# Expert matmuls that read their moving columns and write their PSUM columns from last to first

## The chip, the cores and the metric

One NeuronCore of a Trainium2 chip runs the whole kernel in one launch. The metric is device time in microseconds (us). Three runs of the kernel before gave 1216.09, 1219.02 and 1219.22 us, median 1219.02.

## What is computed

Three layers follow each other over 8 x 576 = 4608 tokens of 512 features:

```python
kv = einsum('bhsd,bhse->bhde', softmax(k, axis=2), v)
x = einsum('bhsd,bhde->bhse', softmax(q, axis=-1), kv)      # linear attention, 8 heads of 64
top2 = the two largest of 8 noisy gate logits of each token
for e in range(8):                                          # mixture of experts
    h = maximum(x[mask] @ w1[e], 0)                         # 512 -> 1024
    out[mask] += top2_w[mask, None] * (h @ w2[e])           # 1024 -> 512
soft mixture of experts over out (32 slots, 8 experts)      # the last layer
```

Everything comes in and goes out as float32. The change touches the two products of the mixture of experts, `x @ w1[e]` and `h @ w2[e]`.

## The kernel before

The attention runs first, and its second half is mixed with the first expert blocks by a table of steps. The last layer (`tail`) stands behind the experts. Between them lies the expert stage: tokens are gathered by expert, in blocks of two or three pieces of 128 tokens that share one expert. `block(b, ...)` does one block in eight units `u`: units 0 to 3 are the first product (a quarter of the 1024 hidden columns each), units 4 to 7 the second (a quarter of its contraction each). In this data there are 35 blocks: 10 early pair blocks, 5 blocks of three pieces ("three-blocks", inside `tc.If`, for which the program holds 14) and 20 further pair blocks.

The products are computed nearly in float32 by splitting. Each operand is stored as a float32r part "h" and a rest "l" (`xh`, `xl`; `hh`, `hl`; `R0h`, `R0l` and so on for three buffers of weights), and each product is three matmuls: h with h, h with l, l with h. The split of a unit's weights (line 797, one ACT activation and one DVE subtraction over 1024 columns) runs two units ahead of their use, from a ring of float32 loads (`ringS`).

Three functions issue the matmuls; in each, the second argument is the stationary operand, which TensorE loads (PEld), and the third the moving one, of which it takes one column after another and writes one PSUM column for each:

- `hidden` (line 830): per unit 24 matmuls; the stationary operand is a 128 x 128 piece of weights, the moving one 256 token columns of `xh` or `xl`, the output half of a bank of `ph`. ACT (line 833) and DVE (line 834) then read `ph` to make `hh` and `hl`.
- `hidden1` (line 843), for the third piece of a three-block: 12 matmuls per unit with 128 tokens stationary and 256 columns of weights moving, the output one half of a bank of `ph`. The result goes through ACT and two transposes (line 849).
- `result` (line 860): the hidden values are stationary, 512 columns of weights move, the output is a whole bank of `py`. A pair block issues 12 matmuls per unit, a three-block 18. DVE (line 865) reads `py`, and an indirect DMA adds the rows to the output.

`xpose` (line 815) transposes the next block's gathered rows into a bank of `ph` in unit 6. All matmuls stand in one queue in program order. The banks of `ph` take turns, and an instruction that reuses a bank waits on semaphores of the engines that used it before; `PE_49` is the semaphore that TensorE's own instructions raise, `DVE_49`, `Activation_49` and `DMASWn_49` those of the others.

```python
for c in range(4):
    for (i, x) in ((0, xh), (0, xl), (1, xh)):
        nc.tensor.matmul(ph[:, g, :], w[i][:, c, g * P:(g + 1) * P], x[:, c, :], start=n == 0, stop=n == 11)
```

Of the kernel before, what the change touches and what calls it, by code (L numbers as in the profile page):

```python
# [21 lines left out]
P = 128  # L22
# [722 lines left out]
def experts(k, att, rs):  # L745

    nc, tc = k.nc, k.tc
    with ExitStack() as ctx:
# [6 lines left out]
        def bank(n, shape):  # L755
            b = banks[n]
            b.append(b.pop(0))
            return b[-1][0].tile(shape, F32, name=b[-1][1])
# [63 lines left out]
        def hidden(b, u):  # L822

            w = [x.rearrange("p (c f) -> p c f", c=4) for x in slot[b, u]]
            ph = bank("ph", [P, 2, 256])
            for g in range(2):
                n = 0
                for c in range(4):
                    for (i, x) in ((0, xh), (0, xl), (1, xh)):
                        nc.tensor.matmul(ph[:, g, :], w[i][:, c, g * P:(g + 1) * P], x[:, c, :], start=n == 0, stop=n == 11)  # L830
                        n += 1
            fs = slice(2 * u, 2 * u + 2)
            nc.scalar.activation(hh[:, fs, :], ph, AF.Relu)  # L833
            nc.vector.scalar_tensor_tensor(hl[:, fs, :], ph, 0.0, hh[:, fs, :].bitcast(F32), op0=ALU.max, op1=ALU.subtract)  # L834

        def hidden1(b, u):

            w = [x.rearrange("p (c f) -> p c f", c=4) for x in slot[b, u]]
            ph = bank("ph", [P, 2, 256])
            n = 0  # L840
            for c in range(4):
                for (i, x) in ((0, x3[0]), (0, x3[1]), (1, x3[0])):
                    nc.tensor.matmul(ph[:, 0, :], x[:, c, :], w[i][:, c, :], start=n == 0, stop=n == 11)
                    n += 1
            hr = yp.tile([P, 256], F32, name="hr")
            nc.scalar.activation(hr, ph[:, 0, :], AF.Relu)
            pt = bank("pt", [P, 4, P])
            for g in range(2):
                nc.tensor.transpose(pt[:, g, :], hr[:, g * P:(g + 1) * P], k.ident)
            fs = slice(2 * u, 2 * u + 2)  # L850
            nc.scalar.activation(h3[0][:, fs, :], pt[:, 0:2, :], AF.Copy)
            nc.vector.tensor_sub(h3[1][:, fs, :], pt[:, 0:2, :], h3[0][:, fs, :].bitcast(F32))

        def result(b, u, py):
            w = [x.rearrange("p (c f) -> p c f", c=2) for x in slot[b, u]]
            order = [(f, s) for f in range(2) for s in range(len(py))]
            for f, s in order if u < 7 else sorted(order, key=lambda x: x[1]):
                a = [x[:, 2 * (u - 4) + f, s * P:(s + 1) * P] for x in (hh, hl)] if s < 2 else [x[:, 2 * (u - 4) + f, :] for x in h3]
                for (n, (h, i)) in enumerate(((0, 0), (0, 1), (1, 0))):
                    nc.tensor.matmul(py[s], a[h], w[i][:, f, :], start=u == 4 and f == n == 0, stop=u == 7 and f == 1 and n == 2)  # L860

        def scatter(b, s, py):
            y = yp.tile([P, D], F32, name="y", bufs=3)
# [8 lines left out]
        def block(b, n_s, n, n_n):  # L872
# [8 lines left out]
            for u in range(8):  # L881
                split(*ahead[u])
                if u == 0:
                    load(n, 0)
                    load(n, 1)
                if u < 6:
                    load(n, ahead[u][1])
                if u < 4:
                    hidden(b, u)
                    if n_s == 3:  # L890
                        hidden1(b, u)
                else:
                    if u == 4:
                        py = [bank(f"py{s}", [P, D]) for s in range(n_s)]
                    if u == XU:
                        for s in range(n_n):
                            xpose(n, s)
                    result(b, u, py)
                if u == 1:
                    finish()  # L900
                    nc.vector.tensor_copy(gc, gn)
                yield
# [501 lines left out]
```

## Time and profile before

| | |
|---|---|
| Median of three runs | 1219.02 us (1216.09 to 1219.22) |
| Profiled execution, its own time | 1222.69 us |
| Its span, first to last instruction | 1221.0 us |
| Granted TensorE clock, mean | 0.967 |
| PE busy | 1125.1 us (92%) |
| DVE busy | 799.3 us (65%) |
| ACT busy | 570.8 us (47%) |
| POOL busy | 324.6 us (27%) |
| HBM traffic | 240 GB/s over the span |

The profiled execution took 1.69 us more than its span and 3.67 us more than the median of the runs. "PE" is the matmul itself and "PEld" the load of the stationary operand, which overlaps it. The duration of one matmul in the records runs from its first column to the modelled end of its last, so back-to-back matmuls overlap in the records; what a matmul costs in a stream is the distance from start to start, which the pieces of the chain give (length of a piece over its count).

### The profile page before, as it was taken

To read this page: it belongs to the slowest core of one execution; us is meant where nothing else is said; L and a number is where in the kernel's file an instruction comes from. 1 tells how busy PE (TensorE), PEld (TensorE's weight loads), DVE (VectorE), ACT (ScalarE), POOL (GpSimd) and SP (SyncE) were. 2 spreads that over 40 slices of the span, in tenths; PEclk is the share of its full clock that TensorE was granted. 3 is DMA by queue.
4 is the path that set the end of the run, shared out by engine and by line. 5 is a ranking of instruction groups with operands and counts; after the bars stand their busy time and mean duration, and the time that the engine had idled before them with its cause. 6 is when DMAs were issued, how large, how long until landed. Compare 5 with 4: busy or idle time off the path is not lost. (4 is left out here: it accounts for less than half of the span.)

```text
span 1221.0 us, 21167 instructions
## 1 busy us (share of the span) xinstructions
PE 1125.1 (92%) x7804; PEld 984.7 (81%) x7804; DVE 799.3 (65%) x1383; ACT 570.8 (47%) x877; POOL 324.6 (27%) x348
## 2 busy tenths in 40 slices
PE   2898859999999999999989999999999999969994
PEld 1787759998889999888968998998998998956542
DVE  7899778666976665554546666666666666645653
ACT  3575355465544544334434454544454454424324
POOL 4442153222244222211223322322321321210000
PEclk8899779999999999999999999999999999988997
DMA  9998162875536566555667564563745253237797
GB/s 327 297 318 306 45 207 77 242 227 157 141 84 189 135 199 172 139 149 163 174 184 249 138 202 106 150 195 84 223 110 173 47 148 84 43 66 295 265 356 310
DMA packets 116104, 219.08 MB, mean 179 GB/s; under 512 B 13968, under 2 KB 54032, under 8 KB 111888
## 3 DMA queue, kind: packets, MB, share of 16 engines
q1 hardware_dynamic: 98944, 177.11, 42.3%
q0 software_dynamic: 17040, 40.44, 16.8%
q8 instruction: 67, 1.10, 0.4%
q14 instruction: 53, 0.43, 0.1%
HBM read 243.31 MB, written 49.70 MB: 240 GB/s over the span
## 5 line engine op out<-in xcount | busy, mean ns | idle before, releaser
L797 DVE TENSOR_TENSOR R1l<-ringS,R1h 128x1024 fp32r<-128x1024 f32 x96 | 117.8, 1227 | 105.8 <-ACT R1h L797 103.3
L797 DVE TENSOR_TENSOR R0l<-ringS,R0h 128x1024 fp32r<-128x1024 f32 x95 | 116.8, 1229 | 100.8 <-ACT R0h L797 100.5
L797 ACT ACTIVATE R1h<-ringS 128x1024 fp32r<-128x1024 f32 x96 | 101.9, 1061 | 144.3 <-PE py L860 85.1
L797 DVE TENSOR_TENSOR R2l<-ringS,R2h 128x1024 fp32r<-128x1024 f32 x91 | 112.0, 1231 | 84.1 <-ACT R2h L797 81.7
L797 ACT ACTIVATE R0h<-ringS 128x1024 fp32r<-128x1024 f32 x95 | 100.8, 1061 | 137.9 <-PE py L860 77.0
L797 ACT ACTIVATE R2h<-ringS 128x1024 fp32r<-128x1024 f32 x91 | 96.5, 1061 | 136.2 <-PE py L860 75.1
L830 PE MATMUL ph<-xl,R0h 128*128 128x256 f32 x400 | 111.7, 279 | 1.5 <-issue 1.5
L830 PE MATMUL ph<-xh,R0h 128*128 128x256 f32 x400 | 112.0, 280 | 1.0 <-DVEq L949 1.0
L830 PE MATMUL ph<-xh,R0l 128*128 128x256 f32 x400 | 111.5, 279 | 0.0
L834 DVE SCALAR_TENSOR_TENSOR hl<-ph,hh 128x512 fp32r<-128x512 f32 x140 | 95.7, 684 | 23.2 <-ACT hh L833 23.2
L830 PE MATMUL ph<-xh,R1h 128*128 128x256 f32 x360 | 101.1, 281 | 8.1 <-DVE sc L820 7.6
L742 POOL DMA_INDIRECT xg<-xtab,pl_idx x40 | 50.3, 1257 | 215.9 <-DVE sc L820 197.6
L830 PE MATMUL ph<-xh,R2h 128*128 128x256 f32 x360 | 100.9, 280 | 0.5 <-DVE hl L834 0.5
L830 PE MATMUL ph<-xl,R1h 128*128 128x256 f32 x360 | 100.7, 280 | 0.0
L830 PE MATMUL ph<-xh,R1l 128*128 128x256 f32 x360 | 100.5, 279 | 0.0
L830 PE MATMUL ph<-xl,R2h 128*128 128x256 f32 x360 | 100.5, 279 | 0.0
L830 PE MATMUL ph<-xh,R2l 128*128 128x256 f32 x360 | 100.3, 279 | 0.0
L866 POOL DMA_INDIRECT x<-y,pl_idx x40 | 64.1, 1602 | 127.9 <-DVE y L865 117.8
L833 ACT ACTIVATE hh<-ph 128x512 fp32r<-128x512 f32 x140 | 81.6, 583 | 31.7 <-PE ph L830 31.7
L860 PE MATMUL py<-R1l,hh 128*128 128x512 f32 x200 | 79.7, 398 | 0.0
L860 PE MATMUL py<-R1h,hl 128*128 128x512 f32 x200 | 79.0, 396 | 0.0
L830 PEld LDWEIGHTS ph<-xh,R0h 128*128 128x128 f32 x400 | 75.7, 189 | 2.3 <-issue 1.6
(441 smaller groups left out, 3011.0 us busy)
## 6 DMA issues: line engine op xcount, KB each, us to landing
ringS<-in_moe_w_dram SPq DMA_DIRECT2D x292, 512.0 KB
ringA<-in_moe_w_dram SPq DMA_DIRECT2D x12, 1024.0 KB
ringA<-in_moe_w_dram SPq DMA_DIRECT2D x22, 512.0 KB
xtab<-xr SPq DMA_DIRECT2D x36, 256.0 KB
kt<-in_k_dram SPq DMA_DIRECT2D x8, 1024.0 KB
v<-in_v_dram SPq DMA_DIRECT2D x8, 1024.0 KB
x<-z SPq DMA_DIRECT2D x5, 1280.0 KB
ringS<-x SPq DMA_DIRECT2D x5, 1024.0 KB
```

The source lines that it names most:

```text
L742: k.nc.gpsimd.indirect_dma_start(out=x, out_offset=None, in_=k.xtab[:n], in_offset=bass.IndirectOffsetOnAxis(ap=idx, axis=0))
L797: turn[1:] = [nc.scalar.activation(r[0], f, AF.Copy), nc.vector.tensor_sub(r[1], f, r[0].bitcast(F32))]
L830: nc.tensor.matmul(ph[:, g, :], w[i][:, c, g * P:(g + 1) * P], x[:, c, :], start=n == 0, stop=n == 11)
L833: nc.scalar.activation(hh[:, fs, :], ph, AF.Relu)
L834: nc.vector.scalar_tensor_tensor(hl[:, fs, :], ph, 0.0, hh[:, fs, :].bitcast(F32), op0=ALU.max, op1=ALU.subtract)
L860: nc.tensor.matmul(py[s], a[h], w[i][:, f, :], start=u == 4 and f == n == 0, stop=u == 7 and f == 1 and n == 2)
L866: d = nc.gpsimd.indirect_dma_start(out=k.x2[:NTOK // 2] if b < NPA else k.x2, out_offset=bass.IndirectOffsetOnAxis(ap=at(b, s), axis=0), i ...
```

## The change

All operands keep their places, sizes and types, and no instruction is added to the products or taken away. In the three functions the moving operand and the output get a step of -1 along the columns: column 255 (or 511) of the moving operand enters first and is written to PSUM column 255 (or 511), and so on down to column 0. Both being turned, every value lands where it did. The stationary operands, the transposes and all readers of PSUM are as before. In the built program these operands start at column 255 (or 511) with a step of -1.

```diff
@@ hidden, line 830
-                        nc.tensor.matmul(ph[:, g, :], w[i][:, c, g * P:(g + 1) * P], x[:, c, :], start=n == 0, stop=n == 11)
+                        nc.tensor.matmul(ph[:, g, ::-1], w[i][:, c, g * P:(g + 1) * P], x[:, c, ::-1], start=n == 0, stop=n == 11)
@@ hidden1, line 843
-                    nc.tensor.matmul(ph[:, 0, :], x[:, c, :], w[i][:, c, :], start=n == 0, stop=n == 11)
+                    nc.tensor.matmul(ph[:, 0, ::-1], x[:, c, :], w[i][:, c, ::-1], start=n == 0, stop=n == 11)
@@ result, line 860
-                    nc.tensor.matmul(py[s], a[h], w[i][:, f, :], start=u == 4 and f == n == 0, stop=u == 7 and f == 1 and n == 2)
+                    nc.tensor.matmul(py[s][:, ::-1], a[h], w[i][:, f, ::-1], start=u == 4 and f == n == 0, stop=u == 7 and f == 1 and n == 2)
```

The order of the instructions is the same on all five engines. What the tracking of dependences adds are waits of TensorE on its own semaphore, four in each three-block and none elsewhere. On PE, in a three-block, the first matmul of `hidden` in unit 2 follows the last two of `hidden1` of unit 1:

```order
 L843 MATMUL ph_4576<-R1h,x3l 128x256
 L843 MATMUL ph_4576<-R1l,x3h 128x256
-L830 MATMUL ph_4600<-xh,R2h 128x256
+L830 MATMUL ph_4600<-xh,R2h 128x256 [waits PE_49]
 L830 MATMUL ph_4600<-xl,R2h 128x256
 L830 MATMUL ph_4600<-xh,R2l 128x256
```

The new wait is for the last matmul of `hidden1` of unit 0, which used the same bank; 38 matmuls lie between it and the waiting one. Unit 3 has the same.

On PE, in unit 6 of a three-block, the first transpose into a bank of `ph`:

```order
 L860 MATMUL py_4702<-R1l,h3h 128x512
 L860 MATMUL py_4702<-R1h,h3l 128x512
-L815 MATMUL ph<-ident,xg_1731 128x128 [waits DMASW3_49]
+L815 MATMUL ph<-ident,xg_1731 128x128 [waits DMASW3_49,PE_49]
 L815 MATMUL ph<-ident,xg_1731 128x128 x3
 L815 MATMUL ph_4753<-ident,xg_1737 128x128 [waits DMASW4_49,DVE_49]
```

Here the wait is for the last matmul of `hidden1` of unit 2, more than 50 matmuls earlier, and since the instruction now waits for two semaphores, one of the waits stands in an instruction of its own ahead of it. The transposes of the third piece have the same.

Waits of this kind stand in the program before as well. On PE, at the start of `hidden1` of unit 0 in the same block:

```order
L830 MATMUL ph_4499<-xh,R0l 128x256
L843 MATMUL ph_4526<-R0h,x3h 128x256 [waits PE_49,Activation_49]
L843 MATMUL ph_4526<-R0h,x3l 128x256 [waits DVE_49]
L843 MATMUL ph_4526<-R0l,x3h 128x256
L843 MATMUL ph_4526<-R0h,x3h 128x256
```

This piece is the same before and after.

## Rows read from the trace of the kernel before

**Rows 1.** The page: busy time, share, instructions; granted clock in 40 slices.

```profile
PE 1125.1 (92%) x7804; PEld 984.7 (81%) x7804; DVE 799.3 (65%) x1383; ACT 570.8 (47%) x877; POOL 324.6 (27%) x348
...
PEclk8899779999999999999999999999999999988997
```

**Rows 2.** Busy time by stretch of 100 us, columns named in the second line.

```profile
core 0: us, PE busy (x) PEld busy (x) DVE busy (x) ACT busy (x) POOL busy (x), PEclk, DMA share, GB/s
200.00:300.00 100.00, 99.75 (x670) 89.47 (x670) 66.10 (x113) 50.94 (x80) 30.66 (x35) 1.00 0.70 209
700.00:800.00 100.00, 100.00 (x663) 90.88 (x663) 64.70 (x89) 49.76 (x62) 26.26 (x24) 1.00 0.58 167
900.00:1000.00 100.00, 100.00 (x665) 90.94 (x664) 65.48 (x91) 48.59 (x60) 27.86 (x21) 1.00 0.45 111
```

**Rows 3.** The chain that ended last, by time: start, length, what, count.

```profile
734.94 5.54 PE py L860 x24
740.48 10.88 PE ph L830 x96
...
757.78 5.56 PE py L860 x24
763.34 11.21 PE ph L830 x96
...
778.12 2.31 PE py L860 x10
...
786.54 11.31 PE ph L830 x96
797.86 3.25 PE py L860 x14
801.43 2.33 PE py L860 x10
```

**Rows 4.** Groups of PE by shape: count, busy us, mean ns, idle before.

```profile
L830 PE MATMUL ph<-xh,R0h 128*128 128x256 f32 x400 | 112.0, 280 | 1.0 <-DVEq L949 1.0
...
L830 PE MATMUL ph<-xl,R2h 128*128 128x256 f32 x360 | 100.5, 279 | 0.0
L860 PE MATMUL py<-R1l,hh 128*128 128x512 f32 x200 | 79.7, 398 | 0.0
...
L860 PE MATMUL py<-R2l,hh 128*128 128x512 f32 x180 | 71.9, 400 | 0.0
...
L843 PE MATMUL ph<-R0l,x3h 128*128 128x256 f32 x40 | 11.7, 292 | 0.0
...
L843 PE MATMUL ph<-R2l,x3h 128*128 128x256 f32 x20 | 6.0, 302 | 0.0
...
L860 PE MATMUL py<-R1h,h3h 128*128 128x512 f32 x20 | 7.9, 396 | 0.0
...
L860 PE MATMUL py<-R0h,h3h 128*128 128x512 f32 x10 | 4.0, 396 | 0.0
```

**Rows 5.** PE by time from 334 us: matmuls whose moving operand has step 2.

```profile
334.74 1.44 PE L506 MATMUL pk<-oa,ob 128*128 128x288 f16 x10
```

**Rows 6.** The chain in the tail: plain float32 matmuls and transposes.

```profile
1112.75 0.87 PE pt L1051 x8
...
1159.09 7.03 PE pq L1289 x64
```

**Rows 7.** PE by time at the start of `hidden1` in a three-block.

```profile
440.87 0.28 PE L830 MATMUL ph<-xh,R0l 128*128 128x256 f32 x1
440.99 0.28 PE L843 MATMUL ph<-R0h,x3h 128*128 128x256 f32 x1
441.11 0.28 PE L843 MATMUL ph<-R0h,x3l 128*128 128x256 f32 x1
```

**Rows 8.** Line 815: minimum, median and maximum ns of its instructions.

```profile
L815 PEldq EVENT_SEMAPHORE  x67: 51/51/536, 169.6 to 1077.5; - x67
```

## The prediction, made before the change was run

> **What bounds the kernel now.** I began with the page's busy times: PE leads with 1125.1 us, DVE follows with 799.3 [rows 1]. That is a mean over three layers, so the second view was busy time by stretch. [...] The third view, the chain that ended last, shows the price of a matmul in the stream. Pieces of 24 matmuls of line 860 last 5.54 to 5.56 us, so 231 ns for 512 columns; pieces of 96 of line 830 last 10.88, 11.21 or 11.31 us, so 113.3 to 117.8 ns, on the mean of the three 116.0 ns, for 256 columns [rows 3]. Both are near 0.45 ns per column. (The 280 and 398 ns in the groups are lengths of single records that overlap; only their counts are used.)
>
> **How many there are.** Line 830 has nine groups, three of 400 and six of 360: 3360. Line 843 has nine, three of 40 and six of 20: 240. Line 860 has nine of whole pairs, three of 200 and six of 180, and nine of the third piece, three of 20 and six of 10: 1800 [rows 4]. So 3600 matmuls of 256 columns and 1800 of 512 are turned around. One ns more on each is 5400 ns = 5.4 us, 0.44% of the run. This kernel is a fine scale for a change of a matmul's price.
>
> **The change, part by part.**
>
> *Reading from last to first.* No matmul here reads downwards. The nearest row is line 506: its moving operand is 288 float16 columns at a step of 2, so 4 bytes from one to the next, like float32 columns. Ten of them take 1.44 us; less the 0.16 us by which the last record outlives its own columns (280 less 116 ns, the same as for line 830) that is 1.28 us, 128 ns each, 0.444 ns per column [rows 5]. Line 830 at its best, step 1, takes 113.3 / 256 = 0.443. A pattern that is not the plain one costs nothing in reading, and I take zero. A step of -1 touches the same words as a step of 1, in the other order.
>
> *Writing from last to first.* All PSUM writes of the trace go upwards with step 1, so the price must be bounded. One end is zero. The other is a matmul that gets through a column in twice the time, as the plain float32 ones do: 8 transposes of 128 columns in 0.87 us are 109 ns each, 0.85 ns per column, and line 1289's 64 matmuls of 512 columns, four side by side, in 7.03 us are 439 ns for each four, 0.86 per column [rows 6]. At 0.85 a 256-column matmul costs 217.5 ns (101.5 more than 116.0) and a 512-column one 435 (204 more than 231): 3600 x 0.1015 + 1800 x 0.204 = 365 + 367 = 732 us. I take zero, because the nearest row, line 506, shows a pattern generator that doesn't care for the step, and because a descending run touches the same pairs of neighbours. This is the weak point of the forecast.
>
> [...]
>
> *The new waits.* Four per three-block, of which five run (line 843's 240 matmuls are 5 x 48): 20. Each is for a matmul at least 38 matmuls, some 4.4 us, earlier, so it is met when PE reaches it. The same kind of wait already stands at the start of `hidden1` in unit 0: its first matmul starts 0.12 us after the one ahead, as the next does after it [rows 7]. Ten waits come as instructions of their own, at 51 ns [rows 8]; even if nothing hid them that is 0.5 us, 0.04%. PE's running stream covers them, so: zero. Were a wait for the matmul just ahead, it would cost 280 less 116 = 164 ns, 20 times 3.3 us; the order excludes that.
>
> *Behind PE.* ACT and DVE start to read `ph` and `py` when the last column is written, which is as late as before. Nothing else changes.
>
> **Sum.** 1222.69 us of the profiled execution + 0. The runs' median lies 3.67 us lower; I forecast that no change is seen against it: 1219.0.
>
> **The forecast's own width.** Line 830's pieces come in two paces in one execution, 113.3 and 117.8 ns [rows 3], with the same instructions. Something outside the matmul picks the pace, and the turned order may pick otherwise. All at 113.3 and line 860 at line 506's 0.444 ns per column (227 ns) would give 3600 x 2.7 ns + 1800 x 4 ns = 17 us less: 1202. All at 117.8 and line 860 at 233 (2.33 us for 10) give 3600 x 1.8 + 1800 x 2 = 10 us more: 1229. A measurement of this kernel can tell about 0.3% (3.7 us) from no change.
>
> **The rivals.**
>
> 1. *PSUM writes at half rate* (slower). Place: the write of every turned matmul. Price: 732 us, 1951 in all. It decides if the write path joins two neighbouring columns only in ascending order. For it: float32 columns at 0.44 ns come twice as fast as in the plain float32 matmuls, so some path may depend on joining. Against it: the pair of neighbours is the same in both orders, and line 506's reads show no such care. Chance 0.17.
>
> 2. *A lost tick now and then* (slower). A tick is the 0.41 ns between 0.85 and 0.44 per column. If one column in four paid one, a 256-column matmul would cost 26 ns more and a 512-column one 52: 3600 x 0.026 + 1800 x 0.052 = 187 us, 1406 in all. Against it, line 506 steps through its operand by the same 4 bytes without such a loss [rows 5]. Chance 0.07. [...]
>
> 3. *The other pace* (either sign), by the bounds above: faster by over 0.3% 0.08, slower by 0.3 to 0.8% 0.09.
>
> 4. *The change doesn't do what it says*: excluded, since the built program has start 255 or 511 and step -1.
>
> **How the numbers follow.** Forecast within 0.3%: 0.58. Faster 0.08, slower 0.09 by the other pace, 0.07 for the lost tick, 0.17 for half rate, and 0.01 for dearer mechanisms. So faster 0.08, same 0.58, slower 0.34. The range runs from 1202, the lower bound of the pace, to 1410, which takes in the lost tick; half rate and worse are left out, 0.18. The likeliest case's own range is 1202 to 1229.
>
> **What would show it.** Right: pieces of 96 of line 830 still last 10.9 to 11.3 us and 24 of line 860 5.5 to 5.6; the stretches of the expert stage look the same. Half rate: some 20.9 us and 10.4 us for these pieces, records longer by about 100 and 200 ns, DVE and DMA shares falling in the stage while PE stays full. A lost tick: about 13.6 and 6.8 us. Waits that count: gaps ahead of the first matmul of `hidden` in units 2 and 3 and of the transposes of the five three-blocks only, none elsewhere. The forecast is wrong if the pace per column in pair blocks, where no instruction and no wait is new, leaves 0.44 to 0.46 ns.

## The result and the profile after

The changed kernel takes 1234.97 us (median of four runs, 1234.08 to 1237.35) against 1219.12 us of the kernel before: ratio 1.0137, 95% interval 1.0113 to 1.0160. It is slower by 15.9 us, 1.4%. The forecast of no visible change was wrong, though the time lies in the stated range; it lies above 1229, the upper end for the likeliest case. The median of the kernel before varied from 1219.12 us here to 1221.42 beside the runs below, so the loss is known to some 2 us only.

The page of the profile after: busy times and granted clock, with the execution's span of 1235.6 us.

```profile
span 1235.6 us, 21177 instructions
...
PE 1139.9 (92%) x7804; PEld 993.4 (80%) x7804; DVE 799.5 (65%) x1383; ACT 571.0 (46%) x877; POOL 326.6 (26%) x348
...
PEclk9899779999999999999999999999999999988997
```

PE is busy 14.8 us longer with the same 7804 matmuls; DVE, ACT and POOL work as long as before [rows 1]. The clock is granted in the same slices but for the first. So the matmuls themselves got dearer.

Busy time by stretch, columns as in rows 2:

```profile
700.00:800.00 100.00, 100.00 (x660) 90.59 (x659) 63.20 (x89) 48.48 (x61) 30.75 (x28) 1.00 0.56 147
900.00:1000.00 100.00, 100.00 (x640) 89.48 (x639) 62.96 (x88) 48.01 (x60) 24.18 (x18) 1.00 0.40 96
```

PE is full as before, at full clock, and gets through fewer instructions in 100 us: 640 where it was 665 in the later stretch (a stretch holds more or fewer of the long ones, so the counts don't give the size).

The chain that ended last, three consecutive blocks and the start of the next; start, length, what, count:

```profile
740.43 5.64 PE py L860 x24
746.07 11.36 PE ph L830 x96
757.43 3.27 PE py L860 x14
...
761.03 2.34 PE py L860 x10
...
763.91 5.68 PE py L860 x24
769.59 11.35 PE ph L830 x96
...
793.10 11.41 PE ph L830 x96
...
811.02 5.64 PE py L860 x24
```

Against [rows 3] a piece of 96 of line 830 takes 11.35 to 11.41 us where it took 10.88, 11.21 or 11.31, on the mean of three blocks 118.5 ns per matmul for 116.0. The pieces of line 860 grew from between 5.54 and 5.58 us to 5.64 or 5.68 per 24, from 2.31 or 2.33 to 2.34 per 10, from 3.25 to 3.27 per 14: about 235 ns per matmul for 231. This is 2% and 1.5%, far from half rate (20.9 and 10.4 us) and from a tick lost on every fourth column (13.6 and 6.8).

How long the stage lasts can be read from one group of line 860, with its first and last start (before, then after):

```profile
L860 PE MATMUL py<-R1h,hh x200: 390/395/498, 204.5 to 1080.4; 128*128 128x512 f32 x100
```

```profile
L860 PE MATMUL py<-R1h,hh x200: 395/399/501, 204.6 to 1092.0; 128*128 128x512 f32 x100
```

The group begins at the same time and ends 11.6 us later. Its shortest record grew from 390 to 395 ns. The other 3.0 us of the longer span lie behind that last start (140.6 us before, 143.6 after), where but for the last matmuls of line 860 the code is unchanged.

Below, a pace in ns "from the starts" is the mean distance of neighbouring starts within one line of the code in the trace, at full clock, leaving out the gaps into which a transpose falls: line 830 went from 115.9 to 118.55, line 860 from 231.35 to 234.6. 3360 x 2.6 + 240 x 1.4 (line 843) + 1800 x 3.3 ns = 8.7 + 0.3 + 5.9 = 15 us. In the late pair blocks the paces account for all of it. Before, three of them last from 734.94 us [rows 3] to

```profile
804.30 5.55 PE py L860 x24
```

which is 69.36 us; after, they last from 740.43 to 811.02, 70.59 us. That is 0.41 us more per block, and 96 x 2.6 + 48 x 3.3 ns are 0.41. For the whole stage the sum is some 3 us more than the 11.6 seen, in part because the trace before has a single wait, behind the last three-block, that the trace after lacks:

```profile
619.60 0.28 PE L830 MATMUL ph<-xl,R0h 128*128 128x256 f32 x1 [1.50 <-issue]
```

So the paces give 15 us, but that this nearly equals the 15.9 us between the medians is partly chance.

### The profile page after: what moved, and what is told of

It is laid out like the page before. It is cut to its first block, busy times and chain, and to the rows that moved or that the text cites. A ratio compares the mean times of both kernels' runs of the same rounds, so it can differ in the third digit from the quotient of the medians.

```text
span 1235.6 us, 21177 instructions
## 1 busy us (share of the span) xinstructions
PE 1139.9 (92%) x7804; PEld 993.4 (80%) x7804; DVE 799.5 (65%) x1383; ACT 571.0 (46%) x877; POOL 326.6 (26%) x348
## 5 line engine op out<-in xcount | busy, mean ns | idle before, releaser
L797 DVE TENSOR_TENSOR R1l<-ringS,R1h 128x1024 fp32r<-128x1024 f32 x96 | 117.8, 1227 | 109.3 <-ACT R1h L797 104.6
L860 PE MATMUL py<-R1h,hh 128*128 128x512 f32 x200 | 78.1, 405 | 0.0
```

The lines of the kernel that those rows point to most:

```text
L797: turn[1:] = [nc.scalar.activation(r[0], f, AF.Copy), nc.vector.tensor_sub(r[1], f, r[0].bitcast(F32))]
L860: nc.tensor.matmul(py[s][:, ::-1], a[h], w[i][:, f, ::-1], start=u == 4 and f == n == 0, stop=u == 7 and f == 1 and n == 2)
```

## The experiments

All ratios are to the kernel before, run beside them on the same chip, with their 95% intervals.

### Which side costs: reading or writing

**Reading alone.** The moving operands are turned, the outputs not, so that the columns of each product come out in reversed order.

```diff
-nc.tensor.matmul(ph[:, g, :], w[i][:, c, g * P:(g + 1) * P], x[:, c, :], start=n == 0, stop=n == 11)
+nc.tensor.matmul(ph[:, g, :], w[i][:, c, g * P:(g + 1) * P], x[:, c, ::-1], start=n == 0, stop=n == 11)
```

and the same in lines 843 and 860.

> Only the moving operand is read from last to first; PSUM is written upwards, so the outputs of the products have their columns in reversed order and the result is not the reference's. No added wait. Theory A (the price lies in reading the moving columns downwards): the whole loss of the change, ratio 1.011 to 1.016, pieces of 96 matmuls of line 830 at 11.36 to 11.41 us and of 24 of line 860 at 5.64 to 5.68. Theory B (it lies in writing PSUM downwards): ratio within 0.3% of 1, pieces 10.9 to 11.3 and 5.54 to 5.56. Theory C (reader and writer must run the same way or else both lose): slower than the change itself.

**Writing alone.** The complement: `ph[:, g, ::-1]`, `ph[:, 0, ::-1]`, `py[s][:, ::-1]`, the moving operands upwards.

> Only PSUM is written from last to first; the moving operand is read upwards, so the products' columns come out reversed and the result is not the reference's. The twenty added waits of the three-blocks are in. Theory A (reading): within 0.3% of before, pieces of 96 of line 830 at 10.9 to 11.3 us, of 24 of line 860 at 5.54 to 5.56. Theory B (writing): ratio 1.011 to 1.016, pieces 11.4 and 5.66. If the added waits cost anything it shows here, in the five three-blocks alone; at most 4 us.

Measured: reading alone 1.0084 (1.0054 to 1.0113), writing alone 1.0006 (0.9987 to 1.0026). The chain of the run that only reads downwards:

```profile
642.29 5.68 PE py L860 x24
647.97 11.41 PE ph L830 x96
665.89 5.64 PE py L860 x24
671.53 11.36 PE ph L830 x96
```

and of the run that only writes downwards:

```profile
640.18 5.58 PE py L860 x24
645.76 11.31 PE ph L830 x96
...
669.06 10.88 PE ph L830 x96
...
691.91 11.21 PE ph L830 x96
```

The first has the change's pieces, the second those of before, in the same sequence of three. From the starts: 118.54 and 234.7 ns for reading down, 115.93 and 231.4 for writing down. Theory A holds, B and C fall. The total of reading alone is less than the change's and than the 1.011 to 1.016 expected (the intervals touch at 1.0113), although the pieces are equal. In its trace the group above starts at 201.9 and ends at 1088.0 us, 886.1 us for 887.4 with the change and 875.9 before, so 10.2 of the change's 11.5 us are in it. The rest of the difference lies outside that stretch, and in the kernel before, which took 2.3 us more beside these runs (1221.42 for 1219.12).

The run that writes downwards holds the twenty added waits, and the one that reads downwards none. With the change there are ten more of these instructions of their own, still at a median of 51 ns [rows 8]:

```profile
L815 PEldq EVENT_SEMAPHORE  x77: 51/51/525, 168.9 to 1089.1; - x77
```

Writing alone shows no loss with them: the waits cost nothing that can be seen.

### Do the two lines add up

**Only lines 830 and 843 turned**, both ways, line 860 as before:

> Lines 830 and 843 turned both ways as in the change, line 860 as before. From the pieces of the two traces the 3600 matmuls of 256 columns lose 118.5 - 116.0 = 2.5 ns each, 9.0 us: ratio 1.007. If the price is per matmul of any width it is 3600/5400 of 15.6 us, 10.4 us (1.0085); if it is per column (1,843,200 columns of all in equal parts) half, 7.8 us (1.0064). Line 860 keeps 231 ns unless the paces of the two lines hang together.

**Only line 860 turned**, both ways:

> Line 860 turned both ways as in the change, lines 830 and 843 as before. By the pieces the 1800 matmuls of 512 columns lose 235.1 - 231.4 = 3.7 ns each, 6.7 us: ratio 1.0055; line 830 should keep its two paces of 113.3 and 117.8 ns. With the run before, the two losses should add up to the change's 15.6 us; a sum far from it would mean that the paces of the two lines hang together.

Measured: 1.0060 (1.0042 to 1.0079), so +7.6 us, where 7.8 to 10.4 us were expected; and 0.9990 (0.9973 to 1.0008), where 1.0055 was expected. The two together are far from 15.9 us. The chain of the second:

```profile
664.12 5.64 PE py L860 x24
669.76 10.88 PE ph L830 x96
687.13 5.68 PE py L860 x24
692.80 10.90 PE ph L830 x96
```

Line 860 has the change's pieces, but line 830, which nobody touched, now runs at 10.88 to 10.90 us in 17 of the 18 late pair blocks that the chain holds, where before it did so in one block of three (6 of 18). From the starts, line 830 went from 115.9 to 114.3 ns: 3360 x 1.6 = 5.5 us back, against 1800 x 3.4 = 6.1 us lost. So the pace of line 830 isn't a property of its matmuls alone; it also hangs on what runs ahead of them.

The starts of each unit of 24 matmuls show the same in the kernel before. In the late pair blocks each of the three weight buffers has units at 113.3 to 113.5 ns and units at 117.7 to 118.0 (12 and 12 for R0, 12 and 12 for R1, 6 and 19 for R2), with the same operands at the same addresses. With the change each buffer has one pace: R0 and R1 117.7 to 117.9, R2 119.9 to 120.0. So for R0 and R1 the turned order took away the faster of two paces that were there already, and only R2 went beyond the slower one.

### What about the read is dear: the step or the walk

**Groups of four down.** Columns go in groups of four (16 bytes), the groups from last to first, the four inside upwards, on both sides.

```diff
-x[:, c, :]
+x[:, c, :].rearrange("p (a b) -> p a b", b=4)[:, ::-1, :]
```

and the same for the output and in the other two lines.

> In all three lines the moving columns and the PSUM columns go in groups of four (16 bytes), the groups from last to first, the four inside each upwards. Every value lands as before. Theory L (what costs is that the read walks downwards through memory, against which the four inside don't matter): the change's paces, 118.5 ns per matmul of line 830 and 234.6 of line 860, ratio 1.010 to 1.016. Theory W (what costs is the negative step from word to word): the paces before, 115.9 and 231.4, ratio within 0.3% of 1. A two-level pattern that is itself dear would show as more than 120 and 240 ns.

**The four inside down**, the groups upwards: `[:, :, ::-1]` in place of `[:, ::-1, :]`.

> The complement: groups of four columns in ascending order, the four inside each from last to first, in reading and in writing. Theory L: the paces before, 115.9 and 231.4 ns, with line 830's two levels of 113.3 and 117.8. Theory W: the change's, 118.5 and 234.6, or more.

Measured: 1.0110 (1.0074 to 1.0146) and 1.0013 (0.9996 to 1.0031). Groups of four down:

```profile
669.66 5.64 PE py L860 x24
675.30 11.36 PE ph L830 x96
693.14 5.67 PE py L860 x24
```

The four inside down:

```profile
670.03 10.88 PE ph L830 x96
687.33 5.56 PE py L860 x24
692.89 11.21 PE ph L830 x96
```

Theory L holds. A step of -1 from word to word shows no cost (1.0013); what costs is that the read walks downwards through memory from one group of 16 bytes to the next (1.0110). The two-level pattern of that run shows no price of its own either (10.88 and 11.21 us for 96 of line 830, 5.56 for 24 of line 860, the pieces of before).

### Is it the direction itself, or a meeting with another stream

In the built program `xh`, `xl`, `hh`, `hl` and the weight buffers don't start alike modulo 2048 bytes, because small tiles lie between them: R2 64 bytes below `xh`, R0 and R1 64 above. The edit only changes the order in which tiles are set up:

```diff
         R[2] = [tile(f"R2{h}", [1024]) for h in "hl"]
-        gn, gc = [tile(n, [3], F32) for n in ("gn", "gc")]
         xh, xl = [tile(f"x{h}", [4, 256]) for h in "hl"]
+        R[0] = [tile(f"R0{h}", [1024]) for h in "hl"]
+        R[1] = [tile(f"R1{h}", [1024]) for h in "hl"]
+        gn, gc = [tile(n, [3], F32) for n in ("gn", "gc")]
...
         nb = wp.tile([1, 2], I32, name="nb")
-        R[0] = [tile(f"R0{h}", [1024]) for h in "hl"]
-        R[1] = [tile(f"R1{h}", [1024]) for h in "hl"]
```

Made to the change, and to the kernel before:

> The change, with the two small tiles and the gather buffer that lay between the operands moved behind them, so that xh, xl, hh, hl and all three weight buffers start at the same address modulo 2048 bytes (with the change as it is, R2 starts 64 bytes below xh in that sense and R0, R1 64 above). Theory A1 (the loss is a meeting of two read streams, the moving columns and the stationary operand loaded for the next matmul, so it hangs on where both lie): the difference between R2 (119.8 ns) and R0, R1 (118.0) in line 830 vanishes, all three within 0.3 ns of each other, at a level that may be another. Theory A2 (reading down costs by itself): every buffer keeps its pace, R2 119.8, R0 and R1 118.0.

> The kernel before with the same moved tiles, so the same addresses as the run ahead of it but everything read upwards. Theory A1: line 830's two paces (113.3 and 117.8, mean 115.9) and R2's 228.9 against 232.5 in line 860 change too, since they would be meetings of the same two streams: the three buffers come within 0.3 ns in line 830 and within 1 ns in line 860. Theory A2: they stay as they are. If all blocks came to 113.3 it would be faster than before by some 9 us.

Measured: with the order turned 1.0098 (1.0061 to 1.0136), with the order upwards 1.0037 (1.0021 to 1.0053), so the kernel before itself gets slower by this. The flat layout read down:

```profile
666.09 5.61 PE py L860 x24
671.70 11.36 PE ph L830 x96
689.54 5.61 PE py L860 x24
```

The flat layout read up:

```profile
663.38 5.49 PE py L860 x24
668.86 11.51 PE ph L830 x96
686.76 5.49 PE py L860 x24
692.24 11.51 PE ph L830 x96
```

Read up, all 18 late pair blocks have 11.51 us for line 830, 119.9 ns: slower in this line than with the change (118.5). The sequence of three is gone in both runs, and from the starts the three weight buffers agree within 0.1 ns in line 830 (119.9 each; read down 118.3, 118.3, 118.4). Line 860 became faster, 5.48 to 5.49 us, 229.1 ns. Of theory A1 this much holds: in both directions the pace of line 830 hangs on where the tiles lie (R2 read down from 119.8 ns to at most 118.4, the mean of all three read up from 115.9 to 119.9). That it is the two reads of TensorE that meet is not shown by it. In line 830 of this layout turning the order even gains 1.6 ns, while in line 860 it loses 4.3.

### Other places, and a faster kernel

Three more orders of the same tiles, read up. The first puts the weights 128 bytes below `xh`, modulo 2048, and level with `hh`; the third 160 below `xh` and 64 below `hh`. The second puts them 64 above both, by this edit:

```diff
-        hh, hl = [tile(f"h{h}", [8, 256]) for h in "hl"]
         R = [[None, None] for _ in range(NR)]
-        R[2] = [tile(f"R2{h}", [1024]) for h in "hl"]
-        gn, gc = [tile(n, [3], F32) for n in ("gn", "gc")]
+        xg = []
         xh, xl = [tile(f"x{h}", [4, 256]) for h in "hl"]
-
-        xg = [tile("xg0", [XC], F32)]
-        nb = wp.tile([1, 2], I32, name="nb")
+        hh, hl = [tile(f"h{h}", [8, 256]) for h in "hl"]
+        gn = tile("gn", [3], F32)
+        gc = tile("gc", [3], F32)
+        R[2] = [tile(f"R2{h}", [1024]) for h in "hl"]
         R[0] = [tile(f"R0{h}", [1024]) for h in "hl"]
         R[1] = [tile(f"R1{h}", [1024]) for h in "hl"]
+        nb = wp.tile([1, 2], I32, name="nb")
+        xg.append(tile("xg0", [XC], F32))
         xg.append(tile("xg1", [XC], F32))
```

The first uses the same lines in the order `hh, hl`, `R[2]`, `R[0]`, `R[1]`, `gn`, `gc`, `nb`, `xg0`, `xh, xl`, `xg1`; the third in the order `R[2]`, `R[0]`, `R[1]`, `gn`, `gc`, `hh, hl`, `nb`, `xg0`, `xg1`, `xh, xl`.

> Everything read upwards as before, tiles in another order: modulo 2048 bytes all weight buffers start 128 bytes below xh and level with hh. Theory A1 (the pace of line 830 hangs on where weights and xh lie to each other, that of line 860 on where weights and hh lie): line 860 at 229 ns, as in the flat layout; line 830 at one value for all three buffers, unlike the 120.0 of the flat one; between 113.3 and 117.8. If it is 113.3 for all, some 13 us less than before (1.1%); if 117.8, no gain.

> Read upwards, weights 64 bytes above xh and above hh, modulo 2048. Theory A1: line 830 for all three buffers as R0 and R1 before, 115.6 ns, within 1 ns; line 860 is new, between 227 and 234.

> Read upwards, weights 160 bytes below xh and 64 below hh, modulo 2048. Theory A1: one value for the three buffers in each line again, both new; if only the distance mattered in a smooth way, line 830 would lie near the run with 128 bytes, and line 860 between 229 (level) and 232.5 (128 bytes).

Measured: 1.0054 (1.0037 to 1.0072), **0.9927 (0.9906 to 0.9948)** and 1.0083 (1.0060 to 1.0105). The chain of the second (its lines count one more, so 831 is 830 and 861 is 860):

```profile
657.78 5.51 PE py L861 x24
663.29 10.90 PE ph L831 x96
680.57 5.51 PE py L861 x24
686.08 10.90 PE ph L831 x96
```

All 18 late blocks have 10.90 us. This kernel takes 1211.87 us against 1220.31 of the kernel before beside it, and so is faster than the kernel before and the changed one. From the starts, in the order of the three runs: line 830 at 119.6, 114.2 and 118.6 ns, line 860 at 229.4, 229.9 and 233.0. In line 830 the three buffers agree within 0.6 ns in every one, as expected; the value 115.6 for the second was 1.4 too high. It came from R0 and R1 of the kernel before, which lie as far above `xh` as here; so the distance to `xh` alone doesn't set the pace. The third shows no smooth rule: 160 bytes is near 128 in line 830, but line 860 lies outside the values expected between.

**The best layout, turned.** Lastly the change's edit in that layout:

> The layout of the run with weights 64 bytes above xh and hh, read and written from last to first as in the change. If reading down has a price of its own beside the meeting of the streams, line 830 goes from 114.2 to some 116.8 ns and line 860 from 229.9 to some 233.2, and the time from 1211.9 to some 1227 us. If direction only sets which meetings there are, line 830 takes another of the values seen with other layouts, 113.3 to 120, and may even keep its pace; in the flat layout turning the order took it from 119.9 to 118.3. Line 860 went up to 233.4 to 234.7 in both layouts when it was turned, so 233 to 235 is expected there by either.

Measured: 1.0095 (1.0070 to 1.0121), 1232.07 us. Its chain:

```profile
668.36 5.61 PE py L861 x24
673.97 11.31 PE ph L831 x96
```

From the starts 118.3 and 233.7 ns: line 830 rose by 4.1 and not by 2.6, so the price is not a fixed one: from 0.9927 to 1.0095 the same edit costs about 1.7% in this layout, and from 1.0037 to 1.0098 about 0.6% in the flat one.

| Layout | line 830 up | down | line 860 up | down |
|---|---|---|---|---|
| as given | 115.9 | 118.5 | 231.4 | 234.6 |
| flat | 119.9 | 118.3 | 229.1 | 233.4 |
| weights 64 bytes above | 114.2 | 118.3 | 229.9 | 233.7 |

Read down, the paces are nearly the same in three layouts; read up, line 830 goes from 114.2 to 119.9. So what the change costs is set by how good the layout was when read up: in line 830 a loss of 2.6 ns, a gain of 1.6 or a loss of 4.1, and in line 860 a loss of 3.2 to 4.3 ns in all three.

## Why the prediction was wrong, point by point

**What bounds the kernel** was right. PE is full in the expert stage, 99.75 to 100.00 of 100 us before [rows 2] and 100.00 after in both stretches above, so a price of a few ns came through: 15 us by the starts, 11.6 us of growth in the stage, 15.9 us between the medians. The time lies in the range only because the range ran to 1410 for the lost tick, which fell; that is luck. The scale of 5.4 us for each ns was the right thing to work out, and should have been a warning: a forecast within 0.3% asserted that no matmul changes by even 0.7 ns.

**Reading from last to first** is the step that failed. It was put at zero because line 506, with a step of 2 in float16, costs 0.444 ns per column like line 830 at its best. That row shows a step of 2 at no cost, and the runs agree: the step of -1 inside groups of four cost nothing (1.0013). It can't show what a walk downwards does, since line 506 walks upwards. The forecast took the pattern for the only thing that could matter. The runs showed a price of 2.6 ns for each 256-column matmul and 3.3 for each of 512 in place of zero, for the walk downwards, and a size that hangs on where the tiles lie. The rows hinted at it: line 830 had two paces with the same instructions [rows 3], and the forecast itself said that something outside the matmul picks the pace. That was used as a width, up to 1229, and not followed up.

**Writing from last to first** at zero was right: 1.0006, with the pieces of before. The reason given for it was weak, as the forecast said: line 506 is a row of reading and shows nothing of PSUM writes. The other reason, the pairs of neighbours, and the rival of half rate turn on a joining of two columns in a write; no run shows one. Groups of four written backwards add nothing either: the pieces of that run, 11.36 and 5.64 us, are those of turned reading alone.

**The waits** at zero were right, by the run that has them without the turned reads (1.0006).

**The rivals.** Half rate fell with the first trace, and so did the lost tick on every fourth column; 2.6 and 3.3 ns more per matmul are far from the 26 and 52 ns of that rival. The "other pace" came nearest in kind and in size: R0 and R1 settled at its 117.8 ns. But its bound took 117.8 and 233 ns for the worst that could be; the change gave 118.5 and 235 on average, 120 for R2, and the flat layout 119.9. The bound allowed 0.8%, and it was 1.4%.

**What stays open.** The layouts show that the pace hangs on the place of the tiles to each other: the flat one and the best differ, among `xh`, `hh` and the weights, only in that the weights lie 64 bytes higher (modulo 2048), and line 830 takes 119.9 or 114.2 ns. That two or more accesses meet is the likely reading, but no run shows the meeting itself or which accesses they are. In line 830 the weight buffers are the stationary operand, so the author's guess at the partner of the moving read is the load of the next matmul's weights. It could not be taken away, since each matmul loads its own (7804 of each [rows 1]). ACT and DVE write and read the same buffers in these units, and no run takes their share away. The traces don't settle it: in the late pair blocks, distances in line 830 over which ACT, DVE and POOL all stand still are few, and as long as the others in the flat layout (120.0 ns for 24 of them) but shorter when it is read down (115.8 for 12; the others 118.4). Transfers are a less likely partner by the author's estimate: distances with no DMA packet of this core under way hardly differ from the rest (119.7 and 119.9 ns in the flat layout, 113.8 and 113.5 in the best). The traces show that the pace of line 830, read upwards, moves between 114.2 and 119.9 ns with the place of the tiles alone; that the load is the partner, no run shows. The 3 us behind the stage in the change's trace are not explained either: other traces here have 140 to 144 us from that last start to the end, with and without turned reads.

## What to carry to other kernels

Where TensorE is full for most of the run, compare the distance of the starts with the best that the same matmul reaches anywhere in the trace (here 113.3 ns of 256 columns), and treat the few ns above it as something to win. Here the order in which tiles are set up, which moves them by up to 224 bytes against each other (modulo 2048), moved the time from 0.9927 to 1.0083 without one instruction changed. When a row is to stand for an operation that the trace lacks, ask which property the row shares (the step) and which it lacks (the direction of the walk).

## What the runs showed of the hardware that was not expected

- In these layouts a matmul with its moving operand read downwards took 2 to 4% longer than in the best one read upwards (118.3 against 114.2 ns for 256 columns, 233.4 against 229.1 for 512), while the downward PSUM write showed no cost (1.0006).
- The same matmul read upwards took 114.2 to 119.9 ns for 256 columns on average, depending on where the tiles lie to each other. Of the places tried, level was the worst for line 830 (119.9) and the best for line 860 (229.1).
- The pace of one line hung on the other: before, the same matmuls on the same buffers ran at 113.3 or at 117.8 ns, unit by unit; turning only line 860 brought the untouched line 830 to the faster of the two in 17 of 18 blocks.
